# Chunk 0 of a fused scan and cosine-gated feed-forward kernel: C loaded four tokens to a row, turned for both units at once, and the first steps put in another order

## The chip, the cores and the metric

The kernel runs on one NeuronCore of a Trainium2 chip. Five engines work side by side, each through its own list of instructions: PE (TensorE, matrix products), DVE (VectorE), ACT (ScalarE), POOL (GpSimd) and SP (SyncE, which here only issues DMAs). The metric is the time of one execution in microseconds (us), as the device measures it. Before the change three runs took 377.79, 377.90 and 377.97 us; their median is 377.9 us.

## The reference

The first half is a chunked state-space scan over 4 sequences, 8 heads, 768 tokens, head size 32 and state size 16; the second half is a feed-forward block of width 2048 on the 3072 x 256 result.

```python
log_a = np.log(np.clip(a, 1e-06, 1.0))
for c in range(nc):                       # chunks of the sequence
    cum = np.cumsum(la, axis=-1)
    L = np.exp(cum[:, :, :, None] - cum[:, :, None, :]) * causal
    M = np.einsum('bhin,bhjn->bhij', Cc, Bc) * L
    y_intra = np.einsum('bhij,bhjd->bhid', M, xc)
    y_inter = np.einsum('bhin,bhnd->bhid', Cc, state) * np.exp(cum)[:, :, :, None]
    y[:, :, sl] = y_intra + y_inter
    state = decay_full * state + sum_j(B_j x_j * decay_from_j)
x = y.transpose(0, 2, 1, 3).reshape(B * S, H * D)
h = x @ w_in                              # 256 -> 2048
g = h * np.cos(h)
out = g @ w_out                           # 2048 -> 256
```

The weights arrive as 64-bit floats; the kernel turns them into 32-bit ones itself. The split into chunks is free: the kernel uses chunks of 128 tokens.

## The kernel before

The sequence is cut into 6 chunks of 128 tokens of all four sequences. For every chunk the scan yields `yT`, and then 16 steps follow. Step n has three parts: `first(n)` (four matmuls with `w_in` into a PSUM bank `hp`), the gate (`wind` on ACT and DVE, `gate` on ACT, `gated` on DVE: h times cos h), and `second` (matmuls with `w_out`). Two banks hold `hp`, so `first(n)` waits for `gated(n - 2)`.

Chunk 0 is worked apart, as two units of 64 tokens, so that the feed-forward part can begin early; steps of unit 0 and unit 1 take turns. For a unit k:

- `load_bc` and `load_x` load B, C and x with the token on the partition: a row holds 16 numbers, so that the DMA moves pieces of 64 bytes. B and x go through SP's queue, C through ACT's.
- `spread_a` (PE) spreads the decays over the rows, `decays0` (DVE, a scan) makes the running products `lam`.
- `turn0` turns B and C with four PE transposes; ACT takes them out of PSUM: `cut` writes C twice with half of the heads masked out each time, `take(0)` copies B, `take(1)` copies C.
- `inner` multiplies C with B on PE (`g`), `weights` multiplies that with `lam` on DVE, `finish0` makes `y` on PE and copies it to `yT` on ACT. For unit 1 `finish0` adds the part of the state: `reach0` makes the decays, `weigh_c` on POOL weighs C with them (`rT`). `take_s` copies the state out of PSUM, `add_s1` adds the old state on POOL (three instructions).

The weights come in 16 pieces, eight of `w_in` and eight of `w_out`. `grade` handles a piece on ACT and POOL (magnitude, clip, last bits), `join` on DVE (two instructions) and then on POOL puts the bits together. Step 2j and 2j + 1 need piece j of `w_in`, the `second` of step 2j the piece j of `w_out`. The first piece of `w_in` is graded and joined in two halves (`n=2`).

All is ordered by hand: every engine executes its instructions in the order in which the Python code calls them, from the block that begins with two `fill` matmuls (without use for the result), through `first_steps` (steps 0 to 3, called once), to the loop from step `AHEAD` = 4 on. In the profile, `first` is line L649, `second` L710 in chunk 0 and L748 later, `y` L426, L434 and L444, `inner` L401, the transposes of chunk 0 L370, the cuts L377, ACT's copies L373, the scan L353, `weigh_c` L391, the grading L225, L227 and L228, the joining L241, L243 and L251, `add_s1` L469 and L471.

DMAs issued by SP and by ACT complete through eight counters that the framework hands out in the program's order; an issue whose counter is still in use waits for the DMA that used it last, and what stands behind it on the issuing engine waits too.

Of the kernel before, what the change touches and what calls it, by code (L numbers as in the profile page):

```python
# [8 lines left out]
FP32 = mybir.dt.float32  # L9
# [16 lines left out]
def kernel(  # L26
# [88 lines left out]

    bcs, xrs = {}, {}

    def load_bc(k, which=(0, 1), eng=nc.sync):

        if k not in bcs:  # L120
            both = loads.tile([P, 2, 2, 2, H, N], FP32, tag="bc", name="bc")
            bcs.update({i: both[:, i] for i in range(2)})
        for w in which:
            for s in range(2):
                eng.dma_start(out=bcs[k][s * W:(s + 1) * W, w].rearrange("p q h n -> p (q h) n"),
                              in_=(B, C)[w][2 * s:2 * s + 2, :, k * W:(k + 1) * W, :]
                              .rearrange("b h i n -> i (b h) n"))

# [105 lines left out]

    def join(which, i, es=(0, 1)):


        parts = held.get((which, i), ())
        for e in es[:len(parts)]:
            high, bits, last = parts[e]  # L240
            V.tensor_scalar(out=bits, in0=bits, scalar1=3, scalar2=0x3FFFFFFF,  # L241
                            op0=ALU.logical_shift_left, op1=ALU.bitwise_and)
            V.scalar_tensor_tensor(out=bits, in0=high, scalar=0xC0000000, in1=bits,  # L243
                                   op0=ALU.bitwise_and, op1=ALU.bitwise_or)
            dst = kept(which, i)
            if len(parts) > 1:
                dst = dst[:, :, e * P:(e + 1) * P]
            else:
                bits, last = (ap.rearrange("p (k f) -> p k f", k=dst.shape[1])
                              for ap in (bits, last))  # L250
            G.tensor_tensor(out=dst.bitcast(U32), in0=bits, in1=last, op=ALU.add)  # L251

    load_bc(0, (0,))
    load_bc(0, (1,), nc.scalar)
    fetch("in", 0)
    load_x(0)
    load_bc(1, (0,))
    fetch("in", 1)
# [12 lines left out]
    ACT.activation(const.tile([P, 1], FP32, name="sine"), quarter, AF.Sin)  # L271
    load_bc(1, (1,), nc.scalar)
    V.memset(a0z[:, :, 0:1], 0.0)
# [31 lines left out]
    share_a(0, V, 0, 6)  # L305
    share_a(1, G, 0, H)
    G.memset(along1[:, :, 0:1], 0.0)
    G.tensor_scalar(out=a0[:, 1], in0=a0[:, 1], **clip)
    for p in range(2):
# [3 lines left out]
    G.tensor_copy(out=own.rearrange("p (h n) -> p h n", h=H),  # L313
                  in_=mine.unsqueeze(2).to_broadcast([P, H, N]))
    G.memset(lead, 0.0)
    G.memset(lead[:, :, 0:1], 1.0)
    slot = const.tile([P, 2], FP32, name="slot")
    V.tensor_reduce(out=slot, in_=ident.rearrange("p (k t n) -> p t k n", t=2, n=N),
                    axis=mybir.AxisListType.XY, op=ALU.add)


# [22 lines left out]

    def decays0(k, p):

        if p == 0:
            lams[k] = scan.tile([P, 2, H, W], FP32, tag="lam", bufs=4, name="lam")
        flat = "p h i -> p (h i)"
        parts = spread.pop((k, p))  # L350
        for i, ps in enumerate(parts):
            hs = slice(i * H // len(parts), (i + 1) * H // len(parts))
            V.tensor_tensor_scan(out=lams[k][:, p, hs].rearrange(flat), data0=ps.rearrange(flat),  # L353
                                 data1=unit0[:, hs].rearrange(flat), initial=0.0,
                                 op0=ALU.mult, op1=ALU.add)

    def weigh0(k):
        scs[k] = sc = scan.tile([P, 2 * H, N], FP32, tag="sc0", bufs=1, name="sc0")
        G.tensor_tensor(out=sc, in0=bcs[k][:, 0].rearrange("p q h n -> p (q h) n"),
                        in1=lams[k].rearrange("p q h i -> p (q h) i")[:, :, W - 1:W]  # L360
                        .to_broadcast([P, 2 * H, N]), op=ALU.mult)

    def turn0(k, tps):

        cuts[k] = scan.tile([P, 2, 2, P], FP32, tag="cT2", bufs=1, name="cT2")
        turns0[k] = scan.tile([P, 2, 2, P], FP32, tag="turned", bufs=1, name="turned0")
        of = [tps[0][:, 0:2], tps[-1][:, -2:]]
        for w in (1, 0):
            for p in range(2):
                PE.transpose(of[w][:, p], bcs[k][:, w, p].rearrange("p h n -> p (h n)"), ident)  # L370

        def take(w):
            ACT.copy(out=turns0[k][:, w], in_=of[w])  # L373

        def cut():
            for t in range(2):
                ACT.activation(cuts[k][:, :, t], of[1], AF.Copy, scale=slot[:, t:t + 1])  # L377
        return cut, take

    def reach0(k):  # L380

        ps = bank([P, NB, W + 1], "a_ps", "h")
        PE.matmul(ps, lhsT=own, rhs=along1, start=True, stop=True)
        flat = "p b i -> p (b i)"
        return lambda: V.tensor_tensor_scan(
            out=reach1.rearrange(flat), data0=ps.rearrange(flat),
            data1=lead.rearrange(flat), initial=0.0, op0=ALU.mult, op1=ALU.add)

    def weigh_c(k):
        rTs[k] = t = scan.tile([P, NB, W], FP32, tag="rT", name="rT")  # L390
        G.tensor_tensor(out=t, in0=turns0[k][:, 1].rearrange("p q (s i) -> p (q s) i", s=2),  # L391
                        in1=reach1[:, :, 1:], op=ALU.mult)

    def inner(k):

        gs[k] = g = [pair("g") for _ in range(2)]
        bT, cT = turns0[k][:, 0], cuts[k]
        for p, s, q in ((p, s, 2 * t + q) for t in range(2) for p in range(2) for s in range(2)
                        for q in range(2)):
            ss, r = slice(s * W, (s + 1) * W), slice(32 * q, 32 * q + 32)  # L400
            PE.matmul(g[q // 2][ss, q % 2, p * P:(p + 1) * P].rearrange("p (t i) -> p t i", t=2),  # L401
                      lhsT=bT[r, p, ss], rhs=cT[r, p, :, ss], start=True, stop=True,
                      tile_position=(32 * q, s * W), skip_group_check=True)

    def weights(k, q):
# [3 lines left out]
                for ap in (units[k], lams[k]))  # L409
        V.tensor_tensor(out=m, in0=gs[k][q][:, :, 0:2 * P].rearrange("p k (s i) -> p k s i", s=2),  # L410
                        in1=l, op=ALU.mult)
# [223 lines left out]

    def first(n):
        c, f = divmod(n, NF)
# [8 lines left out]
        for e in range(2):  # L646
            fs = slice((2 * j + e) * P, (2 * j + e + 1) * P)
            for k in range(KT):
                PE.matmul(to_[:, e], lhsT=w_in[:, k, fs], rhs=y[:, k],  # L649
                          start=(k == 0), stop=(k == KT - 1), skip_group_check=True)  # L650

    def wind(n):
# [151 lines left out]
    wide = [pair("a_ps") for _ in range(2)]  # L804
    spread_a(0, 0, (0, 1), wide[0])
    spread_a(0, 1, (0,), wide[1])
    cut0, take0 = turn0(0, [bank([P, 2, P], "tp", "h") for _ in range(2)])
    spread_a(0, 1, (1,), wide[1])
    spread_a(1, 0)
    for p in range(2):  # L810
        decays0(0, p)
    cut0()
    take0(0)
    scan_reach = reach0(1)
    weigh0(0)
    grade("in", 0, n=2)
    inner(0)
    spread_a(1, 1)
    scan_reach()
    for q in range(2):  # L820
        weights(0, q)
    join("in", 0)
    take_s0, _ = finish0(0)
    for p in range(2):
        decays0(1, p)

# [65 lines left out]
    def first_steps():  # L892

        cut1, take1 = turn0(1, [pair("tp")[:, 0].rearrange("p (k i) -> p k i", k=4)])
        cut1()
        take1(0)
        take_s0()
        take1(1)
        first(0)
        inner(1)  # L900
        weigh_c(1)
        weigh0(1)
        fill(bank([P, 4, P], "warm", "o"), 1)
        for q in range(2):
            weights(1, q)
        rest = grade("in", 1, later=True)
        wind(0)
        rest()
        units_of_decay()
        take_s1, add_s1 = finish0(1)  # L910
        join("in", 1)
        first(1)
        gate(0)
        rest = grade("out", 0, later=True)
        gated(0)
        rest()
        wind(1)
        take_s1()
        clips()
        first(2)  # L920
        rest = grade("in", 2, later=True)
        gate(1)
        join("out", 0)
        rest()
        gated(1)
        wind(2)
        first(3)
        rest = grade("out", 1, later=True)
        gate(2)
        join("in", 2)  # L930
        rest()
        gated(2)
        add_s1()
        wind(3)
        second(0)
        rest = grade("in", 3, later=True)
        gate(3)
        join("out", 1)
        rest()
        gated(3)  # L940
        second(1)
        rest = grade("out", 2, later=True)
        join("in", 3)
        rest()

    first_steps()
    rest_of_loads()
    for n in range(AHEAD, NC * NF + LAG):
        c, f = divmod(n, NF)
        if n < NC * NF:  # L950
# [21 lines left out]
            if n not in piece and behind:  # L972
                behind.pop(0)()
            gated(n)
            for do in (*behind, *unsummed):
                do()
# [54 lines left out]
```

## Time and profile before

| What | Value |
|---|---|
| Median of 3 runs | 377.9 us |
| The profiled execution's own time | 377.81 us |
| Its span, first to last instruction | 376.0 us |
| Busy in the span: PE, DVE, ACT, POOL | 365.3, 281.7, 172.7, 215.1 us |
| Granted TensorE clock, mean | 0.998 |
| PE busy in the first 24 us, and from 24 to 60 us | 20.09, 34.61 us |

The span has 1.8 us around it that belong to the execution and to no instruction. A line of the timeline gives the start, the length, the engine, the source line, the operation, the tiles (written <- read), the sizes and how many instructions are merged in it; in brackets stands the idle time of that engine ahead of it and what ended it. A line of the busy table gives a stretch of the span, its length, the busy time and instruction count of each engine, the granted clock, the mean share of the 16 DMA engines that was busy, and the bytes moved in GB/s. In the DMA view a line gives a queue (q1 is SP's, q10 ACT's, q8 brings instructions), the packets that began in the stretch, the megabytes, and the time that the packets took as a share of 16 engines.

### The profile page before, as it was taken

Reading aid. Unit: us, or ns where it says so; the run is one execution under the profiler, and the core shown is the slowest. Engines: PE = TensorE matmul, PEld = TensorE weight load, DVE = VectorE, ACT = ScalarE, POOL = GpSimd, SP = SyncE. Lnnn points to the kernel's source line nnn. Section 1 sums busy time; section 2 is a strip of 40 time slices with the busy share of each in tenths; the row PEclk is TensorE's granted clock in tenths of the full one; section 3 lists DMA queues with packets and bytes.
Section 4 is the critical chain, followed back from the end, with each engine's and each line's share of the span. In section 5 each row is a group of like instructions: output and inputs, shape, how many; then the busy total and the mean of one; then the engine's idle time right before and its main releaser. Section 6 shows DMA issues by size and latency. Waiting matters only on the chain.

```text
span 376.0 us, 8691 instructions
## 1 busy us (share of the span) xinstructions
PE 365.3 (97%) x3274; PEld 326.0 (87%) x3274; DVE 281.7 (75%) x471; ACT 172.7 (46%) x295; POOL 215.1 (57%) x336
## 2 busy tenths in 40 slices
PE   8978999999999999999999999999999999999995
PEld 4667887888899899999899998999999989999994
DVE  5958999989889957987767987766887872553553
ACT  3586576444354335344434445434444443444442
POOL 5568664489947545674454693363775344544451
PEclk9999999999999999999999999999999999999999
DMA  9999987415536641745223654211020000010011
GB/s 123 227 272 249 254 210 143 98 14 132 127 84 81 125 109 16 125 114 136 28 42 33 124 140 94 51 16 16 3 40 8 13 17 2 2 28 2 5 26 28
DMA packets 124425, 31.54 MB, mean 84 GB/s; under 512 B 93568, under 2 KB 120288, under 8 KB 124384
## 3 DMA queue, kind: packets, MB, share of 16 engines
q1 hardware_dynamic: 120064, 30.60, 38.3%
q10 hardware_dynamic: 4320, 0.39, 0.9%
q8 instruction: 26, 0.43, 0.5%
q14 instruction: 15, 0.12, 0.1%
HBM read 27.64 MB, written 3.34 MB: 82 GB/s over the span
## 4 chain that ended last, share of the span: by engine, by line
PE 71%; POOL 7%; DVE 7%; SPq 5%; DMA 5%; issue 3%; ACT 1%; POOLq 0%; DVEq 0%; ACTq 0%
PE hp L649 34%; PE o L748 30%; SPq L151 3%; POOL words L685 2%; PE y L588 2%; DMA xr<-in_x_dram 2%; PE g L546 2%; DVE mag L243 1%; DVE mag L241 1%; DMA words<-in_moe_w_out_dram 1%; PE y L581 1%; DVE w L656 1%; POOL gd L691 1%; DVE gT L666 1%; SPq L110 1%
## 5 line engine op out<-in xcount | busy, mean ns | idle before, releaser
L649 PE MATMUL hp<-yT,w_in 128*128 128x256 f32 x768 | 183.4, 382 | 3.8 <-POOL la L838 1.9
L649 PEld LDWEIGHTS hp<-yT,w_in 128*128 128x128 f32 x768 | 139.4, 190 | 23.5 <-issue 5.9
L691 POOL TENSOR_TENSOR gd<-gT 128x256 f32<-128x256 f32 x79 | 59.0, 747 | 99.5 <-DVE gT L666 93.0
L661 ACT ACTIVATE w<-w,quarter 128x512 f32<-128x512 f32 x96 | 69.2, 721 | 78.8 <-DVE w L656 78.8
L656 DVE SCALAR_TENSOR_TENSOR w<-hp,k 128x512 f32<-128x512 f32 x96 | 65.4, 681 | 39.5 <-ACT k L654 39.1
L654 ACT ACTIVATE k<-hp 128x512 int32<-128x512 f32 x96 | 57.1, 595 | 81.2 <-PE hp L649 80.9
L666 DVE TENSOR_TENSOR gT<-hp,w 128x512 f32<-128x512 f32 x96 | 65.2, 680 | 34.5 <-ACT w L661 25.7
L748 PE MATMUL o<-words,gd 128*128 128x128 f32 x474 | 65.9, 275 | 0.0
L748 PEld LDWEIGHTS o<-words,gd 128*128 128x128 f32 x474 | 59.3, 192 | 0.0
L496 DVE TENSOR_TENSOR_SCAN lam<-arow,unit 128x512 f32<-128x512 f32 x40 | 56.8, 1421 | 0.0
L748 PEld LDWEIGHTS o<-w_out,gT 128*128 128x128 f32 x316 | 47.5, 191 | 4.0
L748 PE MATMUL o<-w_out,gT 128*128 128x128 f32 x316 | 48.0, 274 | 0.0
L694 POOL TENSOR_TENSOR gd<-gT,gd 128x128 f32<-128x128 f32 x79 | 44.4, 562 | 6.2
L693 POOL TENSOR_TENSOR gd<-gT,gd 128x128 f32<-128x128 f32 x79 | 44.0, 556 | 6.2
L710 PE MATMUL o<-w_out,gT 128*128 128x256 f32 x128 | 30.2, 380 | 1.2 <-POOL w_out L251 1.2
L567 DVE TENSOR_TENSOR m<-g,lam 128x256 f32<-128x256 f32 x80 | 30.9, 415 | 0.5
L748 PE MATMUL o<-words,gT 128*128 128x128 f32 x158 | 30.6, 275 | 0.0
L748 PE MATMUL o<-w_out,gd 128*128 128x128 f32 x158 | 30.5, 275 | 0.0
L710 PEld LDWEIGHTS o<-w_out,gT 128*128 128x128 f32 x128 | 24.2, 190 | 4.8 <-POOL w_out L251 1.6
L748 PEld LDWEIGHTS o<-words,gT 128*128 128x128 f32 x158 | 24.0, 192 | 0.0
L748 PEld LDWEIGHTS o<-w_out,gd 128*128 128x128 f32 x158 | 24.0, 192 | 0.0
L765 DVE TENSOR_TENSOR sum<-ps,sum 128x256 f32<-128x256 f32 (+1 forms) x27 | 16.7, 645 | 0.6
(104 smaller groups left out, 268.2 us busy)
## 6 DMA issues: line engine op xcount, KB each, us to landing
arow<-a_cut SPq DMA_DIRECT2D x20, 512.0 KB
words<-in_moe_w_in_dram SPq DMA_DIRECT2D x8, 512.0 KB
words<-in_moe_w_out_dram SPq DMA_DIRECT2D x8, 512.0 KB
out_dram<-sum SPq DMA_DIRECT2D x18, 128.0 KB
blocks<-in_B_dram SPq DMA_DIRECT2D x128, 8.0 KB
blocks<-in_C_dram SPq DMA_DIRECT2D x128, 8.0 KB
xr<-in_x_dram SPq DMA_DIRECT2D x14, 128.0 KB
along<-a_all SPq DMA_DIRECT2D x20, 64.0 KB
```

The lines of the kernel that those rows point to most:

```text
L496: V.tensor_tensor_scan(out=lam[c, b][:, hs].rearrange("p h i -> p (h i)"), data0=rows_.rearrange("p h i -> p (h i)"), data1=unit[:, b % 2 ...
L567: V.tensor_tensor(out=m_[js, :, :, is_], in0=g_[js, :, :, is_], in1=l_[js, :, :, is_], op=ALU.mult)
L649: PE.matmul(to_[:, e], lhsT=w_in[:, k, fs], rhs=y[:, k], start=(k == 0), stop=(k == KT - 1), skip_group_check=True)
L654: ACT.activation(k, hp[n], AF.Copy, bias=0.25, scale=INV_2PI)
L656: V.scalar_tensor_tensor(out=w, in0=hp[n], scalar=INV_2PI, in1=k, op0=ALU.mult, op1=ALU.subtract)
L661: ACT.activation(cos, cos, AF.Sin, bias=quarter, scale=TWO_PI)
L666: V.tensor_tensor(out=gT[n], in0=hp.pop(n), in1=cos, op=ALU.mult)
L691: G.tensor_tensor(out=d[:, 0:2], in0=g[:, 1:2].to_broadcast([P, 2, P]), in1=g[:, 3::-3], op=ALU.subtract)
L693: G.tensor_tensor(out=d[:, 2], in0=g[:, 0], in1=d[:, 0], op=ALU.subtract)
L694: G.tensor_tensor(out=d[:, 3], in0=g[:, 2], in1=d[:, 2], op=ALU.subtract)
L710: PE.matmul(o[c, u][:, t], lhsT=g[:, 2 * e + t], rhs=w_out[:, 2 * j + e], start=(j == e == t == 0), stop=(j == NJ - 1 and e == 1), skip_gr ...
L748: PE.matmul(at[q], lhsT=a_[q], rhs=w[q], start=(j == 0 and q in starts), stop=(j == NJ - 1), skip_group_check=True)
```

## The change

- C of chunk 0 (both units) is loaded by eight DMAs on ACT's queue, `load_c`. Partition 16 i + g then holds four consecutive tokens of each head: a piece is 64 numbers, 256 bytes. B of unit 1 moves from SP's queue to ACT's, and C of unit 1, which was there, is part of `load_c`.
- A copy on POOL (`c0`) brings the heads of each of the four tokens together, four transposes turn C for both units at once (`turn_c`), and ACT's copies out of PSUM put the tokens back into order (`of`). B is turned unit by unit (`turn_b`).
- `decays0` is a generator: each part of unit 0's scan is issued as soon as its `spread_a` has been.
- The first piece of `w_in` is graded and joined whole.
- The order of the first steps: `inner` of unit 1 in two halves, one ahead of step 0 and one inside it; `weigh_c` before `weights(0)`; one `fill` less; `join` of `w_out`'s first piece before `first(2)`; `second(0)` directly behind `first(2)`; `add_s1` from step 2 to step 6. The decays of unit 1 (`share_a(1, ...)`) go from POOL to DVE. `reach0` takes its bank from another pair.

```diff
+    both = loads.tile([P, 2, NB * H, N], FP32, tag="bc", name="bc")
+    bs = both[:, 0].rearrange("p (k q h) n -> p k q (h n)", k=2, q=2)
+    c4 = both[:, 1].rearrange("p (h r) n -> p h r n", h=H)
+    def load_c(eng):
+        for i in range(8):
+            k, p, s = i // 4, i // 2 % 2, i % 2
+            eng.dma_start(out=c4[16 * i:16 * (i + 1)].rearrange("p h r n -> p h (r n)"),
+                          in_=C[2 * s + p, :, k * W:(k + 1) * W, :]
+                          .rearrange("h (g r) n -> g h (r n)", r=4))
...
-    load_bc(0, (0,))
-    load_bc(0, (1,), nc.scalar)
+    load_b(0)
+    load_c(nc.scalar)
     fetch("in", 0)
     load_x(0)
-    load_bc(1, (0,))
     fetch("in", 1)
...
     ACT.activation(const.tile([P, 1], FP32, name="sine"), quarter, AF.Sin)
-    load_bc(1, (1,), nc.scalar)
+    load_b(1, nc.scalar)
...
-    share_a(1, G, 0, H)
...
+    c0 = loads.tile([P, 2, 2, 4, 2, N], FP32, tag="blocks", name="c0").rearrange(
+        "p a b c d n -> p (a b c d n)").rearrange("p (r h n) -> p r h n", r=4, h=H)
+    G.tensor_copy(out=c0.rearrange("p r h n -> p h r n"), in_=c4)
...
+    share_a(1, V, 0, H)
...
+    def turn_c():
+        tp = bank([P, 4, P], "tp", "h")
+        for r in range(4):
+            PE.transpose(tp[:, r], c0[:, r].rearrange("p h n -> p (h n)"), ident)
+        def of(k, dst, **v):
+            ACT.activation(dst.rearrange("p q (g r) -> p q g r", r=4),
+                           tp[:, :, k * W:(k + 1) * W].rearrange("p r (q g) -> p q g r", q=2),
+                           AF.Copy, **v)
+        def take(k):
             for t in range(2):
-                ACT.activation(cuts[k][:, :, t], of[1], AF.Copy, scale=slot[:, t:t + 1])
-        return cut, take
+                of(k, cuts[k][:, :, t], scale=slot[:, t:t + 1])
+        return take, of
+    def turn_b(k, tp):
+        for p in range(2):
+            PE.transpose(tp[:, 2 * k + p], bs[:, k, p], ident)
+        return lambda: ACT.copy(out=bTs[:, k], in_=tp[:, 2 * k:2 * k + 2])
...
-    spread_a(0, 0, (0, 1), wide[0])
+    spread_a(0, 0, (0,), wide[0])
+    scans = [decays0(0, p, 2) for p in range(2)]
+    next(scans[0])
+    spread_a(0, 0, (1,), wide[0])
+    next(scans[0])
     spread_a(0, 1, (0,), wide[1])
-    cut0, take0 = turn0(0, [bank([P, 2, P], "tp", "h") for _ in range(2)])
+    next(scans[1])
+    take_c, of_c = turn_c()
+    tp_b = bank([P, 4, P], "tp", "h")
+    take_b = turn_b(0, tp_b)
     spread_a(0, 1, (1,), wide[1])
-    spread_a(1, 0)
-    for p in range(2):
-        decays0(0, p)
-    cut0()
-    take0(0)
+    next(scans[1])
+    take_c(0)
+    take_b()
     scan_reach = reach0(1)
     weigh0(0)
-    grade("in", 0, n=2)
-    inner(0)
-    spread_a(1, 1)
+    grade("in", 0)
+    for t in range(2):
+        inner(0, t)
+    take_b = turn_b(1, tp_b)
+    take_c(1)
+    take_b()
     scan_reach()
+    weigh_c(1, of_c)
+    spread_a(1, 0)
     for q in range(2):
         weights(0, q)
     join("in", 0)
     take_s0, _ = finish0(0)
+    inner(1, 0)
+    spread_a(1, 1)
...
     def first_steps():
-        cut1, take1 = turn0(1, [pair("tp")[:, 0].rearrange("p (k i) -> p k i", k=4)])
-        cut1()
-        take1(0)
         take_s0()
-        take1(1)
-        first(0)
-        inner(1)
-        weigh_c(1)
+        first(0, lambda: inner(1, 1))
         weigh0(1)
-        fill(bank([P, 4, P], "warm", "o"), 1)
...
         wind(1)
-        take_s1()
-        clips()
+        join("out", 0)
         first(2)
         rest = grade("in", 2, later=True)
         gate(1)
-        join("out", 0)
+        take_s1()
         rest()
         gated(1)
+        second(0)
         wind(2)
+        join("in", 2)
         first(3)
...
-        add_s1()
         wind(3)
-        second(0)
+        join("out", 1)
...
             gated(n)
+            if n == AHEAD + 2:
+                add_s1()
```

## The prediction

> **What bounds the kernel now.** I read four views: busy times by stretch, the chain that ended last, the timeline of the first 38 us, and the DMA view of single microseconds.
>
> ```profile
> core 0: us, PE busy (x) PEld busy (x) DVE busy (x) ACT busy (x) POOL busy (x), PEclk, DMA share, GB/s
> 0.00:24.00 24.00, 20.09 (x347) 12.05 (x348) 15.80 (x34) 12.90 (x30) 14.08 (x34) 1.00 1.04 220
> 24.00:36.00 12.00, 10.82 (x51) 9.21 (x50) 9.42 (x13) 8.39 (x15) 9.73 (x12) 1.00 0.90 235
> 36.00:60.00 24.00, 23.79 (x113) 20.51 (x112) 23.57 (x31) 15.20 (x27) 14.97 (x16) 1.00 0.87 216
> ```
>
> After the first 36 us TensorE is never idle for long, so what the change is worth is the moment from which TensorE runs without gaps. DVE is nearly full too from 36 to 60. The timeline has the marks that I count from:
>
> ```profile
> 13.33 1.97 PE L649 MATMUL hp<-yT,w_in 128*128 128x256 f32 x8 [0.19 <-ACT yT L454]
> 17.00 0.98 PE L426 MATMUL y<-rT,state 32*64 32x64 f32 x32
> 23.44 3.61 PE L649 MATMUL hp<-yT,w_in 128*128 128x256 f32 x16 [1.88 <-POOL la L838]
> 33.41 1.99 PE L710 MATMUL o<-w_out,gT 128*128 128x256 f32 x8 [1.18 <-POOL w_out L251]
> ```
>
> These are: step 0 of `w_in` (13.33), unit 1's `y` (17.00, called Y below), step 2 of `w_in` (23.44), and step 2 of `w_out` (33.41). From 33.41 on, groups of four matmuls follow each other every 1.73 us (33.41, 35.24, 36.97, 38.70), with only 0.21 and 0.23 us of idle time at 49.50 and 60.76. The chain says what the head waits for: `4.22 7.11 DMA xr<-in_x_dram`, x of unit 0, issued at 4.22 and there at 11.33.
>
> **Where C arrives.** This is the term that decides, and the trace of before has no such load. Before, C of unit 0 is two DMAs with 64-byte pieces, issued by ACT at 0.74. Afterwards C of both units is eight DMAs on ACT's queue, 128 pieces of 256 bytes each, 1,024 packets in place of 4,096. The built program gives each DMA one of eight completion counters, and a counter is used again only when its last DMA has landed. So ACT's fourth C waits for its first, the fifth for the first half of B on SP's queue, the sixth and seventh for the second and third, the eighth for the fourth. One POOL copy waits for all eight. Such waits are real in the trace: ACT's last C of before is issued at 4.22, 2 us after the one ahead of it, because it shares a counter with the first C, and SP's second pair of B at 4.97 shares one with the first half of B.
>
> So: ACT issues three at 0.74 to 2.1 (an issue takes 0.40 to 0.47 by the rows of `a` and `a_in`), the fourth at about 2.9, the fifth when B's first half is there. That was 4.97; without half of C in front (1,024 packets at the 1,500 to 1,750 a microsecond of the busiest windows) about 4.4. Four issues at 0.44 end at 6.2. If a DMA then takes what `a` took (issued 0.74, used at 2.52: 1.78), the last one, issued at 5.8, is there at 7.6. That is the early end.
>
> The late end comes from the order in which the queues are served:
>
> ```profile
> q1 hardware_dynamic: 870, 0.29, 115.0%
> q10 hardware_dynamic: 30, 0.00, 2.1%
> ```
>
> ```profile
> q1 hardware_dynamic: 744, 0.09, 84.8%
> q10 hardware_dynamic: 1004, 0.06, 72.0%
> ```
>
> These are the packets of 7 to 8 us and of 8 to 9 us; q10 is ACT's queue. ACT's C piece issued at 4.22 moves nothing to speak of until 8, when SP's `w_in` and first half of x, issued at 2.73 and 3.58, are through. A DMA issued on ACT queues behind what SP issued earlier. Afterwards x is issued at 3.58 and 4.22 still, ahead of the fifth C. With 3,072 packets fewer (1.9 us at 1,600 a microsecond) x would be there at 9.4 rather than 11.33, and the fifth to eighth C just behind it or beside it. I take 9.3 for all of C. If ACT's issues also block as SP's did (the pair of B at 4.97 took 4.52 us to issue), it is 11. Ends 7.6 and 11; I take the value that the row of 4.22 supports, as it is the same queue at the same moment.
>
> The Trainium skill, "DMA: Bandwidth & Descriptors", section "Queues, rings and completion order", states that each DMA engine takes turns between the queues that have work. By that rule ACT's C would not wait for SP's x, C would be there at the early end, and the total would come out at 378.0. The two windows above speak against it, and I go by them.
>
> **From C to Y.** The POOL copy into head order, 128x512, is bounded by L831's 0.61 and the split copy L289's 0.88: 0.65. Four transposes 0.66 to 0.91: 0.8. Two cuts 0.84 and the copy of B 0.37 on ACT. With 0.1 for each of three hand-offs, ACT has them done at 9.3 + 0.65 + 0.8 + 1.21 + 0.3 = 12.3 (before: 7.74). Then ACT in program order: both halves of the grading as whole instructions 0.72 + 0.71, unit 1's two cuts 0.84, B's copy 0.37, `c1` 0.40: 3.05. `weigh_c` on POOL now stands in front of the join of `w_in` and waits for `c1`: 0.68, then the whole join 1.27 (19.05's row; before it was two of 0.72, the first of them over at 12.60). With hand-offs 5.2 us after 12.3, step 0 of `w_in` starts at 17.5, not 13.33: +4.2.
>
> Part is given back, since half of unit 1's inner products, its first scan and its spreads now run before that. From step 0 to Y it takes only step 0 (1.73) and the other half of the inner products (0.40 of 0.80): 2.1 in place of 3.67. Y is at 19.6, 2.6 later.
>
> **From Y to the gapless stretch.** Step 2 and step 3 of `w_in` ran before step 0 of `w_out`; now `w_out` follows step 2 at once, so its piece 0 sets the pace. Before, DVE's part of that join ended at 23.98 and POOL's followed a grading of 1.10, ending at 25.68. The grading now stands behind it: 23.98 + 1.27 = 25.27, that is Y + 8.3. The 1.88 us gap at 23.44 therefore costs nothing either way: both waits of that matmul were over at 21.13, an instruction packet was fetched from 20.9 (queue q8), and if the gap stays, step 2 still ends before Y + 8.3. Four groups from there end at Y + 15.2. Piece 1 of `w_out`: step 3 ends at Y + 11.9, then 0.60 + 0.68 (wind), 0.42 + 0.69 (join), 1.27 (POOL) and hand-offs: Y + 15.8. Before it was 33.41 − 17.00 = Y + 16.4, because `add_s1` (1.39 + 0.73) sat in front on POOL. Gain 0.6, with ends 0 (DVE slowed again as at 32.17, 1.48 for 0.42) and 1.2.
>
> **Taken at nothing, and by what.** `add_s1` itself, 2.1 us, moves to step 6, where POOL is busy 14.97 of 24 us; without that cover it costs its 2.1. `share_a` of unit 1 goes from POOL to DVE, about 0.75 (0.56 for three quarters of the size), inside DVE's 2.41 us idle time ahead of 5.93. Unit 0's first scan starts about 1 us earlier, but its fourth now waits behind C's transposes and has 0.5 us to spare against the inner products. The dropped filler, 0.57, lay in TensorE's wait for POOL. SP loses two issues of 4.52 us together, so `w_in`'s second piece is issued near 5.5, not 9.54; ACT did not wait for it at 14.97, so nothing. DVE's lead saves perhaps half of the late idle 0.44: 0.2.
>
> **Sum.** +2.6 − 0.6 − 0.2 = +1.8 on the profiled 377.81 (span 376.0 and 1.8 around it; 0.09 under the median 377.9): 379.6, in terms of the median 379.7.
>
> **Rivals.**
> 1. C comes early and it is faster. Place: the last C piece; price: 1 us per us; it decides at 7.5 us, where the sum is zero. At 6.5 the time is 376.8. For it: 3,072 packets fewer, and the early end 7.6 touches it. Against: the counters alone make 6.2 for the last issue.
> 2. Unit 1's B is later still. It goes to ACT's queue behind eight C, its second half waiting for `w_in`'s landing (8.70 before), and TensorE meets its transposes ahead of unit 0's `y`. From its landing to Y there are 0.5 + 0.5 + 1.5 (y), 0.4, 0.5, 2.1: 5.6. At 13.5 it is hidden; at 15.5 Y is at 21.1 and the time 381.2.
> 3. The delay is made good: DVE, 23.57 of 24 busy, is the real limit from 36 to 60, and the delay comes out of TensorE waits there. Against: those waits are 0.44 us in all, so 1.18 + 0.44 is the most that can come back: 378.0 with luck.
>
> **How the numbers follow.** Forecast 0.5, rival 2 0.2, rival 1 0.2, rival 3 0.1. The low end: C at 7.6 (−1.7), quick hand-offs (−0.2), gain 1.2 (−0.6): 377.2, stretched to 377.0 for part of rival 1. The high end: C at 11 (+1.7), no gain (+0.6), or rival 2: 382.0. About 0.2%, 0.76 us, is what a measurement of this kernel can tell from no change: faster 0.2, same 0.1, slower 0.7.
>
> **What would show it.** In the changed profile: the transposes of C start near 10.1 us and their releaser is POOL's copy; ACT's issues of C stretch to 6 us or beyond; step 0 of `w_in` starts near 17.5, Y near 19.6; step 0 of `w_out` waits for POOL near 28; step 2 of `w_out` waits well under 1.18. I am wrong if C's transposes start before 8.5, if step 0 starts before 15.7, or if TensorE shows new gaps after 36 us (then `add_s1` or DVE is the cause).

## The result and the profile after

The changed kernel takes 395.45 us (median of 4 runs, 394.74 to 398.08); the kernel before, beside it on the same chip, 377.94. The ratio is 1.0474 with a 95% interval of 1.0422 to 1.0526: slower by 17.5 us where 1.8 were forecast. The profiled execution took 394.78 us with a span of 393.0, so 16.97 us more than that of before.

Busy times by stretch, kernel after:

```profile
core 0: us, PE busy (x) PEld busy (x) DVE busy (x) ACT busy (x) POOL busy (x), PEclk, DMA share, GB/s
0.00:24.00 24.00, 9.73 (x60) 4.72 (x60) 8.38 (x21) 4.44 (x9) 6.36 (x20) 0.75 0.98 223
24.00:36.00 12.00, 11.51 (x278) 7.04 (x279) 5.74 (x7) 5.31 (x13) 4.95 (x8) 0.78 0.01 3
36.00:60.00 24.00, 21.07 (x94) 17.07 (x93) 18.11 (x27) 16.14 (x30) 15.04 (x17) 1.00 0.74 194
```

TensorE is busy 9.73 us of the first 24 where it was 20.09, all other engines wait too, and the DMA engines are nearly as busy as before (0.98 against 1.04). From 24 to 36 us they move next to nothing: every load issued by then had come. The granted clock, 1.00 before, is 0.75 and 0.78. The timeline of TensorE, kernel after, at the marks of the prediction:

```profile
11.29 1.11 PE L382 MATMUL tp<-ident,c 128*128 128x128 f32 x4 [4.20 <-POOL c L322]
24.03 0.66 PE L397 MATMUL tp<-ident,bc 128*128 128x128 f32 x2 [8.08 <-DMA bc<-in_B_dram]
30.19 1.13 PE L669 MATMUL hp<-yT,w_in 128*128 128x256 f32 x4
32.91 0.69 PE L446 MATMUL y<-rT,state 32*64 32x64 f32 x32
41.07 1.99 PE L732 MATMUL o<-w_out,gT 128*128 128x256 f32 x8 [1.98 <-POOL w_out L258]
48.75 1.99 PE L732 MATMUL o<-w_out,gT 128*128 128x256 f32 x8 [0.51 <-POOL w_out L258]
117.24 1.00 PE L608 MATMUL y<-m,xr 128*32 128x128 f32 x24 [0.34 <-POOL m L580]
```

These are the transposes of C, those of unit 1's B, step 0 of `w_in`, Y, step 0 and step 2 of `w_out`. The last line, a wait for POOL in chunk 1, serves as a far mark: it stood at 100.35 before, so 16.89 of the 16.97 us are lost ahead of it and 15.91 ahead of Y (17.00 before). The two idle times, 4.20 for C and 8.08 for B of unit 1, are new. The far mark in the timeline of TensorE, kernel before:

```profile
100.35 0.89 PE L588 MATMUL y<-m,xr 128*32 128x128 f32 x20 [0.34 <-POOL m L560]
```

The timelines of ACT and POOL, kernel after, say how the loads were issued:

```profile
0.74 6.07 ACTq L133 DMA_DIRECT2D bc<-in_C_dram  x8
10.14 3.14 ACTq L125 DMA_DIRECT2D bc<-in_B_dram  x2
10.62 0.61 POOL L322 COPY c<-bc 128x512 f32<-128x512 f32 x1 [5.24 <-DMA bc<-in_C_dram]
```

and the chain of waits has one piece of 11 us: `12.64 11.26 DMA bc<-in_B_dram`, the second half of unit 1's B, issued by ACT at 12.64 (its counter had been held by an x that landed at 12.62) and there at 23.89. The last C landed at 10.57.

The DMA view of single microseconds, kernel after, from 7 to 8 us and from 20 to 21 us (queue, packets, MB, share of 16 engines; q1 is SP's, q10 ACT's):

```profile
q1 hardware_dynamic: 977, 0.12, 115.2%
q10 hardware_dynamic: 180, 0.04, 35.9%
...
q1 hardware_dynamic: 162, 0.33, 97.7%
q10 hardware_dynamic: 161, 0.01, 14.5%
```

In the second pair both queues moved the same number of packets, but SP's are weights in pieces of 2,048 bytes and ACT's are B in pieces of 64. So beside the stream of weights the 1,024 pieces of B's second half moved at about 170 a microsecond, from 17.1 to 23.9 us. Before that they did not move at all: from 14 to 17 us ACT's queue has no packet, though this half had been issued at 12.64. The DMA view from 15 to 16 us has SP's queue alone:

```profile
q1 hardware_dynamic: 248, 0.30, 109.6%
```

Of the 11.26 us, about 4.5 thus went by while DMAs that SP had issued earlier were moved (weights issued at 11.88 landed by 17.45), and 6.8 in equal turns with the later ones.

### The profile page after: what moved, and what is told of

The parts are those of the page before. It is cut to its first block, busy times and chain, and to the rows that moved or that the text cites. A ratio compares the mean times of both kernels' runs of the same rounds, so it can differ in the third digit from the quotient of the medians.

```text
span 393.0 us, 8684 instructions
## 1 busy us (share of the span) xinstructions
PE 369.1 (94%) x3272; PEld 326.7 (83%) x3272; DVE 281.5 (72%) x470; ACT 172.4 (44%) x293; POOL 215.2 (55%) x334
## 4 chain that ended last, share of the span: by engine, by line
PE 67%; DVE 9%; SPq 8%; DMA 7%; POOL 5%; issue 3%; ACT 1%; DVEq 0%; POOLq 0%; ACTq 0%
PE hp L669 32%; PE o L770 27%; SPq L159 5%; DMA bc<-in_B_dram 3%; PE y L608 2%; DVE mag L250 2%; SPq L110 2%; DVE lam L516 2%; DVE mag L248 2%; POOL words L707 1%; DVE w L678 1%; PE g L566 1%; DMA xr<-in_x_dram 1%; DMA words<-in_moe_w_in_dram 1%; PE y L601 1%
## 5 line engine op out<-in xcount | busy, mean ns | idle before, releaser
L361 DVE TENSOR_TENSOR_SCAN lam<-a_ps,unit 128x256 f32<-128x256 f32 (+1 forms) x6 | 5.1, 864 | 18.5 <-PE a_ps L349 18.5
```

## The experiments

Theory 1 after this: unit 1's B came late, and TensorE, which has its transposes in front of unit 0's `y`, waited for it. Rivals: C's lateness and the new order of steps do most of it, with B only a passenger; or the halved clock does. Marks are those of the profiled executions; "far mark" is the wait for POOL in chunk 1.

**B of unit 1 back on SP's queue.**

```diff
     load_x(0)
+    load_b(1)
     fetch("in", 1)
...
-    load_b(1, nc.scalar)
```

> The changed kernel with one thing undone: B of unit 1 is loaded by SP behind x of unit 0 again, not by ACT behind the eight C. Theory 1 (B of unit 1 is the cause; it landed at 23.89 us and TensorE stood still for 8.08 us in front of its transposes): B lands by 13 us, the idle time of 8.08 us in front of the transposes of B is gone, what stays is C. The sixth to eighth C now wait for counters that w_in's first piece and x use, so C is complete at 11 to 13 us and Y (unit 1's first y, 32.91 in the changed kernel, 17.00 before) comes at 21.5 to 24; time 381 to 385. Rival (the late C and the new order of the head do most of it, B is only a passenger): Y stays above 28 and the time above 389.

Measured: 389.37 us, ratio to before 1.0294 (1.0272 to 1.0315). The idle time for B is gone, Y is at 27.25. But C is now at 14.33: its last loads stand behind counters that `w_in`'s first piece and x use, the last one issued at 9.86 instead of 6.37. The timeline of TensorE in this run:

```profile
15.11 1.12 PE L382 MATMUL tp<-ident,c 128*128 128x128 f32 x4 [8.44 <-POOL c L322]
```

The time is in the rival's range and Y in neither: the undo took B's wait away and lengthened C's, through the shared counters. It shows that both loads matter and does not part them.

**Fillers in TensorE's idle time.** Seven `fill` matmuls ahead of the transposes of B, nothing else.

```diff
+    fill(bank([P, 4, P], "warm", "o"), 7)
     take_b = turn_b(1, tp_b)
```

> The changed kernel with seven more filler matmuls (128x512) on TensorE ahead of the transposes of unit 1's B, in its idle time of 8.08 us; nothing else is changed. B still lands near 23.9. Theory 1 (the granted clock is part of the cost: 0.50 from about 19 to 29.3 us, while TensorE was busy for 5.2 us of it): the clock stays at 1.00 from about 16 to the end of the stretch or comes back before 24, the work from the transposes of B to Y shrinks from 8.9 us to about 6.3, time 392.0 to 393.3. Rival (hand-offs on ACT, DVE and POOL set the pace there, the clock costs nothing): 394.7 to 395.6. If the clock did most of the 17 us the time would fall under 388.

Measured: 395.75 us, 1.0472 (1.0444 to 1.0500): the time did not move. Yet the clock was 1.00 from 16.0 to 39.9 us, and with B there at 23.70, Y came at 30.61, 2.3 earlier. Two later places took it back, both in this timeline of TensorE:

```profile
33.95 3.72 PE L669 MATMUL hp<-yT,w_in 128*128 128x256 f32 x16 [1.51 <-ACT w L683]
39.83 3.68 PE L732 MATMUL o<-w_out,gT 128*128 128x256 f32 x8 [2.16 <-POOL w_out L258]
43.35 1.89 PE L669 MATMUL hp<-yT,w_in 128*128 128x256 f32 x8
```

The fillers moved TensorE's list by 28 instructions, so that the fetch of its next instructions (a q8 packet at 31.09) fell into open work: 1.51 us at 33.95. The profile names ACT as the releaser; but TensorE stops at the same place in its list, behind about 705 matmuls and weight loads, as at 23.44 in the kernel before, and goes on 1.4 to 1.5 us after the packet's end in both. In the changed kernel the packet began at 33.94, and TensorE, which came to that place at 38.3, had no wait there. And the clock fell to 0.50 from 40 to about 43 us, so eight passes took 3.68 instead of 1.99. The local part of theory 1 held, its time did not. Clock alone is not the 17 us.

**B of unit 1 on POOL's own queue.** ACT's and SP's counters up to the last C stay as in the changed kernel.

```diff
-    load_b(1, nc.scalar)
...
+    load_b(1, G)
     c0 = loads.tile(...)
```

> The changed kernel, B of unit 1 loaded through POOL's own queue (issued ahead of the copy of C) and not behind the eight C on ACT; ACT's eight issues and SP's wait for the same counters as in the changed kernel, so that C arrives as there, near 10.6 us. This separates B from C, which the run with B on SP could not: there C came at 14.33. Theory 1 (late B is worth more than the 6 us that run showed, since C came 3.8 us later in it): B lands by 17, the idle time of 8.08 us shrinks below 2, Y comes at 22.5 to 25, time 384 to 388. Rival (the head is bound by C and by the new order, B is worth 6): Y at 26 to 27.5, time 388.5 to 390.

Measured: 389.23 us, 1.0274 (1.0232 to 1.0316). C landed at 11.28, B at 13.50, no idle time for B, Y at 25.34 (timeline of TensorE in this run):

```profile
16.80 0.69 PE L397 MATMUL tp<-ident,bc 128*128 128x128 f32 x2
25.34 0.85 PE L446 MATMUL y<-rT,state 32*64 32x64 f32 x32
```

So B's lateness is worth 7.6 us at Y although C came 0.7 later, and 6.2 of the time: Y lies near theory 1's range, the time in the rival's. In the profiled execution the clock was at 0.50 around 34 to 38 us again, and two groups of eight passes took 2.63 and 2.98 instead of 1.99 and 1.89.

**Weights held back while B is on its way.** Five pieces of weights are issued by SP only behind `clips()`.

```diff
-    for w in (("in", 2), ("out", 1), ("in", 3), ("out", 2), ("in", 4)):
-        fetch(*w)
...
         clips()
+        for w in (("in", 2), ("out", 1), ("in", 3), ("out", 2), ("in", 4)):
+            fetch(*w)
```

> The changed kernel with five later pieces of the weights (w_in 2 to 4, w_out 1 and 2) loaded by SP only behind the two stores of the decays, so that from about 16 us on SP's queue has nothing to move while B of unit 1 is on its way; everything else, ACT's queue too, is as in the changed kernel. The time itself says little, since these pieces come late. Theory (the 64-byte pieces of B's second half, on ACT's queue, landed at 23.89 because SP's stream of weights was served beside them at the same rate of packets): both halves are there by 14 to 17.5, and the idle time of 8.08 us in front of B's transposes falls under 2. Rival (the load of 64-byte pieces is slow by itself, or its late issue decides): the second half still lands at 21 or later.

Measured: B's second half, issued at 13.31, later than the 12.64 of the changed kernel, landed at 17.13, the wait in front of its transposes is 0.53, Y at 25.71. The DMA view of this run from 15 to 16 us:

```profile
q10 hardware_dynamic: 1502, 0.10, 102.7%
q1 hardware_dynamic: 56, 0.02, 8.7%
```

1,502 packets in a microsecond instead of 161: the pieces of 64 bytes are not slow, and the late issue doesn't decide. SP's DMAs, those ahead of them and those beside them, do: here too the two halves, issued at 12.56 and 13.31, moved only 20 packets before 15 us, but then had hardly anything to take turns with. (The total, 393.03 in a single run, includes the wait for the later weights.)

**C turned unit by unit.** ACT issues only the four C of unit 0, SP two B and four C of unit 1 behind x of unit 0; copy and transposes in two halves. Order of steps as changed.

```diff
-    load_c(nc.scalar)
+    load_c(0, nc.scalar)
     fetch("in", 0)
     load_x(0)
+    load_b(1)
+    load_c(1, nc.sync)
...
-            PE.transpose(tp[:, r], c0[:, r].rearrange("p h n -> p (h n)"), ident)
+            PE.transpose(tp[:, r, ss], c0[ss, r].rearrange("p h n -> p (h n)"), ident[ss, ss])
...
+    copy_c(1)
+    turn(1)
     take_b = turn_b(1, tp_b)
```

> The changed kernel with nothing of unit 0 waiting for unit 1: ACT issues only the four C of unit 0, SP the four C and the two B of unit 1 behind x of unit 0, POOL copies and TensorE turns C in two halves of 64 partitions. The rest, the order of the steps too, is that of the changed kernel. Theory (late loads are nearly all of the 17 us): unit 0's C is there at 6.0, its transposes start at 6.7 to 7.2 (11.29 in the changed kernel), unit 1's loads land at 12 to 14.5 and TensorE waits for them in front of unit 1's transposes; Y at 18.5 to 21.5, time 380.5 to 383.5. Rival (the new order, with weigh_c ahead of the join and the joining of w_in's first piece as a whole, costs several us by itself): transposes as early, but Y at 23 or later and time 385 or more.

Measured: 384.88 us, 1.0155 (1.0117 to 1.0193); unit 0's C landed at 5.93, unit 1's loads at 11.46. The timeline of TensorE in this run:

```profile
7.90 0.69 PE L390 MATMUL tp<-ident,c 64*128 64x64 f32 x4
13.07 0.48 PE L390 MATMUL tp<-ident,c 64*128 64x64 f32 x4 [1.43 <-POOL c L326]
16.00 1.04 PE L464 MATMUL y<-m,xr 64*32 64x64 f32 x62
21.68 0.44 PE L456 MATMUL y<-rT,state 32*64 32x64 f32 x10
```

With all loads early Y is still 4.7 us late, between the two expectations. Unit 0's `y` stood at 10.81 before:

```profile
10.81 0.32 PE L434 MATMUL y<-m,xr 64*32 64x64 f32 x8
```

Here it starts at 16.00, since the turning and spreading of unit 1 stand in front of it. (About 1.2 us of that is a slow start of TensorE in this execution: a later run with the same instructions up to the first transposes has them at 6.66 instead of 7.90.) So the loads are not "nearly all". The clock shows here as well: the four runs took 382.14 us at a mean clock of 0.999, 384.14 at 0.995, and 385.63 and 385.95 at 0.989.

**The turning of unit 1 behind unit 0's `y`**, on top of the last one; the join of `w_in`'s first piece then stands ahead of `weigh_c`.

```diff
-    turn(1)
-    take_b = turn_b(1, tp_b)
-    take_c(1)
-    take_b()
     scan_reach()
-    weigh_c(1, of_c)
...
     take_s0, _ = finish0(0)
+    take_c, of_c = turn_c(1, tp_1[:, 0])
+    take_b = turn_b(1, tp_1[:, 1])
+    take_c(1)
+    take_b()
+    weigh_c(1, of_c)
     inner(1, 0)
```

> The run with C turned unit by unit (384.9; Y at 21.68), and on top of it the turning of unit 1 (four transposes of C, two of B, ACT's cuts and copies, weigh_c) moved from ahead of unit 0's y to behind it, so that the join of w_in's first piece no longer stands behind weigh_c on POOL; the other order is that of the changed kernel, steps of w_out included. Theory (the place of unit 1's turning ahead of unit 0's y is what is left of the delay: y started at 16.00 there, 10.81 in the kernel before): unit 0's y starts at 12 to 13.5, Y comes at 17.5 to 19.5, time 379 to 381.5. Rival (the later first transposes, 7.90 against 6.17, and the copy of C on POOL carry the rest through): Y at 20 or later, time 382 or more.

Measured: 385.52 us, 1.0175 (1.0146 to 1.0204). The `y` of unit 0 moved to 12.64 as expected; Y did not move, it is at 22.16. The timeline of TensorE in this run says why:

```profile
16.19 0.67 PE L426 MATMUL g<-cT,turned 32*64 32x128 f32 x16 [1.48 <-ACT c L390]
16.78 1.89 PE L354 MATMUL a_ps<-m,those 128*64 128x512 f32 x4
18.60 1.97 PE L674 MATMUL hp<-yT,w_in 128*128 128x256 f32 x4
```

Half of unit 1's inner products still stands ahead of step 0 of `w_in`, waits for ACT's copies of unit 1, and the clock (at half from 16.9 to 20.3, 0.72 in the mean from 16 to 22) doubles part of what follows. The theory had left this instruction out; the rival's numbers came true, its reason isn't shown. How much of Y is the order and how much the clock is open: in this execution TensorE also ran at half speed until about 10 us, and the next run, with the same instructions up to unit 0's `y`, has that `y` at 10.66, not 12.64.

**All of the old order, the new loads.** As above, and the inner products behind step 0, the steps of `w_out` as before, `add_s1` at step 6.

```diff
-    inner(1, 0)
     spread_a(1, 1)
...
-        first(0, lambda: inner(1, 1))
+        first(0)
+        for t in range(2):
+            inner(1, t)
```

> As the run with unit 1's turning behind unit 0's y, and besides both halves of unit 1's inner products behind step 0 of w_in and the steps of w_out in the order of before with add_s1 at step 6: what is left of the change is C in pieces of 256 bytes, its copy on POOL, the scan part by part, the whole join of w_in's first piece and the late add_s1. Theory (the order of steps, not the load form, made the changed kernel slow): 376.5 to 378.5, Y at 17 to 18.5. Rival (the copy on POOL and the extra DMA issues cost 1 to 3 us in the head wherever they stand): 379 to 381.

Measured: 378.68 us, 1.0011 (0.9990 to 1.0032); 0.2 above the theory's range and below the rival's; step 0 at 14.34, Y at 17.84, the clock 1.00 from 4 to 60 us. The timeline of TensorE in this run:

```profile
17.84 0.33 PE L451 MATMUL y<-rT,state 32*64 32x64 f32 x4 [0.85 <-POOL unit L875]
```

The loss is gone. The new form of C does little harm where its units are loaded and turned apart, and no gain shows: the late `add_s1` that this kernel contains lowers the median by 0.9 alone, as the next runs show, so what else is left of the change may cost as much.

**The steps behind Y, in both kernels.** First the changed order of these steps in the kernel before, and the late `add_s1` alone in it:

```diff
-        add_s1()
...
+            if n == AHEAD + 2:
+                add_s1()
```

> The kernel before with one part of the change: the three instructions of add_s1 go from step 2 to step 6. Theory (add_s1, 1.39 + 0.73 us on POOL, stands in front of the join of w_out's second piece, and step 2 of w_out waits 1.18 us for it): that wait falls to 0 to 0.6, time 376.8 to 377.4. Rival 1 (another wait takes its place, such as DVE's part of the join): 377.6 to 378.1. Rival 2 (POOL has no room at step 6): a TensorE wait of 0.5 us or more between 50 and 62 us, time 378.3 or more.

and then, with it, the other steps in the changed order:

```diff
+        rest = grade("out", 0, later=True)
         take_s1, add_s1 = finish0(1)
...
+        join("out", 0)
         first(2)
...
+        second(0)
         wind(2)
+        join("in", 2)
         first(3)
...
+        second(1)
         wind(3)
+        join("out", 1)
```

> The kernel before with the changed order from unit 1's y on: grading of w_out's first piece ahead of that y, its join ahead of step 2 of w_in, step 0 of w_out directly behind step 2, step 1 of w_out behind step 3, add_s1 at step 6; the loads, the turning and the steps up to there are as before. Theory (this part is the good part of the change, worth 0.6 to 1.2): step 0 of w_out starts near Y + 8.3, step 2 of w_out waits under 0.6, time 376.6 to 377.4. Rival (step 0 of w_out waits for the join of its piece and holds up step 3, so that what is gained later is lost here): 377.8 to 379.

Measured: late `add_s1` 377.32 us beside 378.22 for the kernel before, ratio 0.9989 (0.9968 to 1.0009); with the whole changed order 379.40, 1.0035 (1.0016 to 1.0054). Step 2 of `w_out`, timeline of TensorE, first with `add_s1` alone, then with the whole order:

```profile
32.16 1.99 PE L710 MATMUL o<-w_out,gT 128*128 128x256 f32 x8
```

```profile
24.12 2.38 PE L649 MATMUL hp<-yT,w_in 128*128 128x256 f32 x8 [2.30 <-issue]
35.06 1.99 PE L710 MATMUL o<-w_out,gT 128*128 128x256 f32 x8 [0.46 <-POOL w_out L251]
```

The wait of 1.18 us is gone with `add_s1` alone, though 0.5 of it comes back in waits for gT (0.18, 0.32 and 0.39 against 0.21 and 0.23). The rest of the new order adds 2.1 us to that in the medians, where I had expected a gain. (This profiled execution, 381.01, had the clock at 0.86 from 24 to 36 us, which lengthens its first line to 2.38 and is not part of the 2.1.) Then the reverse in the changed kernel: the lines with a plus above go back to their old places, `add_s1` stays at step 6.

> The changed kernel with the steps from unit 1's y on in the order of before (join of w_out's first piece behind step 2 of w_in, steps 0 and 1 of w_out behind step 3 of w_in), only add_s1 stays at step 6; loads, turning and head as changed. Theory (the new order of these steps costs about 1.2 to 2 us, by the pair of runs of the kernel before, 379.4 against 377.3): step 2 of w_out at most Y + 15.2, the waits for gT between 50 and 100 us under 1.0 in sum, time 393.2 to 394.4. Rival (with TensorE late, the order doesn't matter, since the joins have more time): 395.0 to 395.8.

Measured: 391.81 us, 1.0359 (1.0327 to 1.0392), 3.6 better than the changed kernel, more than either expectation. Y is the same (33.01), step 2 of `w_out` comes at Y + 14.46 instead of Y + 15.84, and the far mark at Y + 81.46 instead of Y + 84.33. TensorE now waits in one place (timeline of this run) and then not again until 70:

```profile
40.49 1.97 PE L669 MATMUL hp<-yT,w_in 128*128 128x256 f32 x8 [1.48 <-DVE gT L688]
42.29 3.62 PE L732 MATMUL o<-w_out,gT 128*128 128x256 f32 x16
```

**`add_s1` later still**, in the kernel before:

```diff
-        add_s1()
...
+            if n == AHEAD + 6:
+                add_s1()
```

> The kernel before with add_s1 at step 10 (the run at step 6 took 377.3, with TensorE waits for gT of 0.18, 0.32 and 0.39 us between 48 and 61 us that the kernel before had as 0.21 and 0.23). Theory 1 (add_s1 at step 6 is what lengthens those waits): they fall to 0.5 in sum, time 376.8 to 377.2. Theory 2 (the waits are DVE's own, in step with the earlier start): the same waits, 377.1 to 377.5. If POOL has no room at step 10 either: a new wait near 65 to 70 us and 378 or more.

Measured: 377.62 us beside 378.48, ratio 0.9975 (0.9958 to 0.9992): 0.9 below the kernel before in the median, with an interval that just leaves out no change. The waits for gT are 0.19 and 0.23, as theory 1 has it, but TensorE's fetch wait is 2.71 in this profile (1.57 with `add_s1` at step 6), and the time is 0.4 above theory 1's range. That steps 6 and 10 differ isn't shown. That moving `add_s1` alone gains is shown for step 10, by 0.3 to 1.6 us; for step 6 the median is 0.9 lower too, but the interval includes no change.

## Why the prediction was wrong

**What the runs add up to.** In medians: B off ACT's queue 6.2 (395.45 to 389.23), C and B of unit 1 out of unit 0's way 4.4 more (to 384.88), the old order of steps 6.2 more (to 378.68), of which the steps behind Y had 3.6 when undone by themselves. These steps depend on each other and are one way to cut the sum. The clock is in it as well: at a mean clock of 0.999 the run with C turned unit by unit took 382.14, 3.5 above the last of these medians, and at 0.989 it took 385.95. So up to about half of the last 6.2 may be half-clock stretches that came with the waits of that order; the runs don't part the two.

**Where C arrives: right mechanism, too small.** C was there at 10.57, forecast 9.3, early end 7.6, late end 11. ACT's later loads waited for the named counters (issues at 2.76, 5.05 and, the last, 6.37 against 2.9, 4.4 and 5.8) and landed behind x, whose second half came at 9.90 instead of 9.4. What stands behind C took 0.9 more than priced: ACT was done at 14.48, not 12.3, and of that the transposes, 1.11 + 0.63 against 0.8, ran at half clock.

**From C to Y: this step failed.** It put step 0 of `w_in` at 17.5 and Y at 19.6; they came at 30.19 and 32.91. The sum followed ACT and POOL and took it for granted that what TensorE has in front of unit 0's `y` would have its data. Rival 2, at 0.2, had nearly all of the mechanism: ACT's queue, behind eight C, the second half waiting for a landing, TensorE meeting the transposes ahead of `y`. What was wrong in it is the term "landing", taken at 13.5 to 15.5 and measured at 23.89. I had looked at when B could be issued and not at what it would then share the DMA engines with. The issue itself came at 12.64, not near 8.70: by then the counter that `w_in`'s first piece had held was held by an x. From there B took 11.26 us. Without its lateness (the run with B on POOL's queue) Y came at 25.34, still 5.7 behind the 19.6, so C, the order of steps and the clock are in the miss as well.

The rule that I had weighed bears on just that. By the measured rows, ACT's queue got 180 of 1,157 packets from 7 to 8 us, and 161 of 323 from 20 to 21. The Trainium skill, "DMA: Bandwidth & Descriptors", section "Queues, rings and completion order", has each DMA engine take turns between the queues with work. The second row agrees; the first doesn't, with eight C issued by 6.37 of which none but the first four had landed, and neither does the stretch from 14 to 17 us without a packet of B. Taking the rule as refuted by one pair of windows was too quick: the second of them, with 744 and 1,004 packets, has x and C moving side by side. Both readings were needed: B's second half stood about 4.5 us behind what SP had issued earlier, as the prediction had read it for C, and then took 6.8 us in equal turns against 2,048-byte pieces. What decides when a later DMA of the other queue begins to move, no run here shows.

**5.6 us from B's landing to Y** took 9.0 (23.89 to 32.91), and 6.9 in the run with fillers, at full clock. So by these two profiles about 2.1 of the miss is the halved clock, which the prediction didn't mention, and 1.3 is work missed in the sum.

**From Y to step 2 of `w_out`: right in its numbers, in part by luck.** Step 0 of `w_out` came at Y + 8.16 (forecast 8.3), step 2 at Y + 15.84 (15.8), with no wait for a fetch, so the gain of 0.6 is there. But with the steps undone and only `add_s1` late, step 2 came at Y + 14.46, and in the kernel before with the late `add_s1` at Y + 14.78 (Y was 17.38). So moving `add_s1` gained about 1.6 us there (0.3 of it a shorter wait for the fetch, 1.57 for 1.88), and the new order of the other steps gave 1.4 of it back.

**The gain of 0.6 + 0.2 in the sum: wrong sign.** From Y to the far mark it took 84.33 us against 83.35 before. What was gained at step 2 came back: 1.28 us of waits for gT between 58 and 78 us, where there had been 0.44. That is near rival 3's remark that DVE limits this stretch, though rival 3 drew another conclusion. That the late `add_s1` costs nothing at its new place was right; the changed order of the other steps was priced as a gain and costs 2.1 in the kernel before.

**What would make it wrong** named new gaps of TensorE after 36 us, with DVE as cause: those appeared. A start of C's transposes before 8.5 us did not.

## What to carry to other kernels

When a load moves to another queue, look not only at when it can be issued but at what streams ahead of it and beside it: pieces of 64 bytes next to 2,048-byte pieces moved at 161 a microsecond, alone at 1,502. An engine works its list in order, so for every instruction that the change puts ahead of the critical one, ask for the arrival of each of its inputs; a late input of unit 1 stopped all of unit 0. And measure parts of a change one by one: here one line, the late `add_s1`, lowered the median of the kernel before by 0.9 us, while the whole change cost 17.5.

## What the runs showed of the hardware that was not expected

**The clock of TensorE falls in the head once it waits.** The kernel before had 1.00 from 5.6 to past 36 us. For the first microseconds the busy table says 1.00 too, but a trace has no record of the clock there, in the kernel before until 5.6 us, in the run with fillers until 16.0. Instruction lengths show half speed in that stretch: eight matmuls took 1.98 us in the run with fillers (its timeline of TensorE) and 1.08 in the changed kernel.

```profile
6.00 1.98 PE L349 MATMUL a_ps<-m,those 128*64 128x256 f32 x8 [0.96 <-DVE lam L361]
```

Single microseconds of the kernel after, in the busy table (the clock is the third number from the end):

```profile
8.00:9.00 1.00, 0.00 (x0) 0.00 (x0) 0.00 (x0) 0.33 (x2) 0.00 (x0) 0.89 1.51 141
...
15.00:16.00 1.00, 0.95 (x33) 0.71 (x32) 0.70 (x1) 1.00 (x4) 0.92 (x2) 0.70 1.10 303
...
19.00:20.00 1.00, 0.00 (x0) 0.00 (x0) 0.00 (x0) 0.00 (x0) 0.00 (x0) 0.51 1.14 345
...
29.00:30.00 1.00, 1.00 (x8) 0.24 (x4) 0.00 (x0) 1.00 (x4) 0.00 (x0) 0.87 0.00 0
```

It halves from about 8.8 to 15.6 and from 19.0 to 29.3 us: 1.7 and 3.1 us after TensorE fell idle (7.1 and 16.0), and it is back 4.3 and 5.2 us after the work resumed (11.29 and 24.03). The Trainium skill, "TensorE: Matmul & The Clock Gate", section "Part 1: The HAM clock gate", gives one window of about 3.4 us, free-running, of idling or of work as the condition; the stretches of 6.8, 3.4 and 10.2 us between the changes are two, one and three such windows, and the 4.3 and 5.2 fit a window that starts at any time; the falls after 1.7 and 3.1 us of idling are shorter than one window (the 3.4 us ahead of the first fall held 1.08 us of matmuls, from 6.00 on), and no run here shows how much idling a window must hold. A wait of 4 us thus cost more than its length, and a filler that saved the clock in one place saw it fall in another.

**An undo can be worse than it looks.** The eight completion counters are dealt out in the order of all DMAs, so putting B back on SP's queue delayed the last issue of C from 6.37 to 9.86.
